# Square roots with a constant offset, two units in one instruction, and new instruction lists in a fused gated-recurrence and soft-MoE kernel

## The chip, the core and the metric

The kernel runs on one core of one Trainium2 chip. The metric is the device time of one execution in microseconds. Of the kernel before, three runs were timed: 292.63, 292.97 and 293.97, with a median of 292.97.

## What is computed

The input is a sequence model's layer followed by a soft mixture of experts. x, r_gate and i_gate are 4 x 5056 x 256 floats, and a_param holds one value per channel.

```python
log_a = 8 * sigmoid(r_gate) * log(sigmoid(a_param))
a_t = exp(log_a)
x_gated = sqrt(maximum(1 - a_t * a_t, 1e-6)) * sigmoid(i_gate) * x
h = a_t[:, t] * h + x_gated[:, t]          # for every t; y[:, t] = h
logits = y @ phi                           # 20224 tokens x 32 slots
slot_input = softmax(logits, over tokens).T @ y
slot_out = relu(slot_input @ w1[e]) @ w2[e]     # 8 experts, 4 slots each
out = softmax(logits, over slots) @ slot_out
```

The softmax over tokens needs all tokens, so the work falls into a first phase over all of them, a short middle (the two expert layers) and a last phase that writes 20.7 MB of output.

## The kernel before

**Tiles.** The 20224 tokens are cut into 40 quads of 512 (the last has 256). Quads are put together in 21 units: quad 0 alone, then pairs, then quad 39 alone. A big buffer, tag "b", holds one unit: 128 partitions (channels) x 2 halves of the 256 channels x 1024 tokens; there are 20 of them, made as ten tiles of two neighbours (line 579). Units are worked off in nine chunks of 2, 2, 3, 3, 3, 3, 2, 2 and 1 (CHUNKS, line 24), because ACT has to load another function table for the square root and batches the roots of one chunk between two loads.

**Steps of the first phase, by task name** (unit p or quad q behind it, and a half of the channels after the dot):

- Dr, Di, Dx: loads, issued by SP (line 728).
- TR: PE turns the r gate round to channels by tokens. SR: ACT takes tanh(r/2) into the buffer A (line 812).
- SI: ACT takes tanh(i/2) in place (line 827). The gate is sigmoid = (1 + tanh)/2, so what follows forms (1 + tanh) x, which is twice the gated input. A letter of IV (line 32) says how for each quad: P adds the 1 on POOL (P1, line 838) and multiplies on DVE or POOL (U, line 850); D does both in one DVE instruction (line 848); E multiplies only, and PE adds the two transposes (TU, line 922) in PSUM.
- EX: ACT takes the exponential of A (line 880), where two units of a chunk stand in neighbouring buffers in one instruction of 2048 elements. SQ: POOL or DVE squares it into N (line 867).
- RT: ACT takes the root of N in place (line 903). Since the gated input is doubled, the root is of (1 - a*a)/4, with an offset that is read from a tile called quarter.
- ST: DVE multiplies the root into the transposed input in PSUM (line 940). SC: DVE's scan along the tokens (line 957). It goes unit after unit, each from where the one before ended.
- TY: PE turns y round again (line 980). YC: DVE or ACT copies it to SBUF (lines 996 and 994).
- LG, LE, LD, TE, ES, AC, AE, DM: logits of a group of up to four quads, the running maximum, exponentials relative to it, the sum of slot inputs, and its rescaling when the maximum grows (lines 1042 to 1131).

**The middle.** merge_tasks (line 1297) brings the four partition blocks' running maxima to one: MT transposes them, MX and MR reduce and replicate, MC transposes back, WJ subtracts, WE takes the exponential, W scales the rows of a matrix R. SP and DN add the blocks up with it, SL and RD copy out and invert the sum. L1 (line 1375) and L2 (line 1423) are the expert layers, 128 matmuls each; HS, HT and HR copy, transpose and rectify between them, for four experts at a time. SO, RS and BD spread the result.

**The last phase.** For each group: CT, CM, CS, CE, RR, RB, RC and CN form the softmax over slots (partly done early), HP and HE turn it round, OT multiplies, OE copies to SBUF on DVE or ACT, OD stores.

**What sets the order.** The order of tasks on each of the five queues is written out by hand in ORDER (line 91). A planner (line 249) replays the lists with estimated durations to decide which buffer each task gets (take, line 473); all waits come from the data and the buffers. Each engine works strictly in the order of its list. Buffers that a double exponential is to use are "mates", which the planner takes together as two free neighbours (twin, line 455).

Of the kernel before, what the change touches and what calls it, by code (L numbers as in the profile page):

```python
# [17 lines left out]
P = 128  # L18
J = 4
# [12 lines left out]
IV = 'PDPDDDEPEPPEPDEPPPEEDEPEEDEDPEPPPPPEDPPP'  # L32
# [74 lines left out]
    ),  # L107
    "ACT": (
# [13 lines left out]
    ),  # L122
# [16 lines left out]
    ),  # L139
    "POOL": (  # L140
# [6 lines left out]
    ),  # L147
# [8 lines left out]
    ),  # L156
}
SWITCH = 0.09
WARMF = 1.4
COLD = 5.6  # L160
COLDB = 0.95
MARGIN = 0.25
COLDT = 3.3
COLDW = 3.4
FEW = 2.0
COLDX = 1.9
LOAD = 1.41

EX2 = True

MI = ()
RT2 = ()
SPR = 1.28
ISSUE = 0.45
AHEAD = 0.96
LATE_DMA = 0.2
PEX = 1.03

ODS = 0


# [24 lines left out]
class Buf:  # L206


    __slots__ = ("tags", "tag", "slot", "users", "name", "need", "late", "mate", "kept")

    def __init__(self, tags, name=""):
        self.tags = tags if isinstance(tags, tuple) else (tags,)
# [8 lines left out]
class Planner:  # L221
# [219 lines left out]
    def tag_for(self, b, taken={}):  # L441
        for g in b.tags:
            if b.kept is not None:
                return g
# [1218 lines left out]
```

## Time and profile before

| | |
|---|---|
| median of three runs | 292.97 us |
| profiled execution: its own time | 292.97 us |
| profiled execution: span from first to last instruction | 291.2 us |
| granted TensorE clock, mean | 0.968 of full speed |
| busy: PE, DVE, ACT, POOL | 253.9, 241.4, 241.4, 180.7 us |
| moved by DMA | 100.07 MB, 79 of them read |
| first output store issued | 237.79 us after the span's start |

All times below are in microseconds from the span's start, if nothing else is said. A row of the timeline joins instructions of one kind that follow one another; "x2" says how many, and the duration runs from the first one's start to the last one's end. In brackets stands how long the engine sat idle before, and what ended that. Successive ACT instructions overlap a little in the rows: the next one's start comes some 0.1 us ahead of the last one's end.

### The profile page before, as it was taken

To read this page: it belongs to the slowest core of one execution; us is meant where nothing else is said; L and a number is where in the kernel's file an instruction comes from. 1 tells how busy PE (TensorE), PEld (TensorE's weight loads), DVE (VectorE), ACT (ScalarE), POOL (GpSimd) and SP (SyncE) were. 2 spreads that over 40 slices of the span, in tenths; PEclk is the share of its full clock that TensorE was granted. 3 is DMA by queue.
4 is the path that set the end of the run, shared out by engine and by line. 5 is a ranking of instruction groups with operands and counts; after the bars stand their busy time and mean duration, and the time that the engine had idled before them with its cause. 6 is when DMAs were issued, how large, how long until landed. Compare 5 with 4: busy or idle time off the path is not lost.

```text
span 291.2 us, 6478 instructions
## 1 busy us (share of the span) xinstructions
PE 253.9 (87%) x2602; PEld 200.1 (69%) x2602; DVE 241.4 (83%) x277; ACT 241.4 (83%) x268; POOL 180.7 (62%) x138
## 2 busy tenths in 40 slices
PE   8997796897989999999998999999999999968620
PEld 7997685676876787777777677777675677746300
DVE  0059999999999999999999999999975558998530
ACT  4999999999999999999999999999842059866400
POOL 4344795798799999969999999997002021130100
PEclk9999999999999999999999999999999999999755
DMA  7999999999999998798859959999993029999996
GB/s 237 409 409 409 410 399 410 405 409 394 344 407 407 356 396 283 270 350 306 288 182 342 308 201 365 369 421 416 424 414 151 2 87 415 411 423 411 420 421 268
DMA packets 23634, 100.07 MB, mean 344 GB/s; under 512 B 2866, under 2 KB 2868, under 8 KB 19636
## 3 DMA queue, kind: packets, MB, share of 16 engines
q1 hardware_dynamic: 23600, 99.66, 88.1%
q8 instruction: 20, 0.33, 0.4%
q14 instruction: 10, 0.08, 0.1%
q10 hardware_dynamic: 4, 0.00, 0.0%
HBM read 78.94 MB, written 20.71 MB: 342 GB/s over the span
## 4 chain that ended last, share of the span: by engine, by line
ACT 39%; PE 27%; DVE 22%; issue 7%; POOL 1%; POOLq 0%; DVEq 0%; ACTq 0%
ACT b L880 9%; ACT b L812 9%; ACT st L827 9%; DVE b L957 8%; DVE pair L940 5%; ACT b L903 5%; PE bank L1590 5%; PE pair L922 3%; PE bank L1423 2%; PE pair L980 2%; ACT L903 2%; DVE b L1604 2%; PE one L1116 2%; DVE yn L996 2%; ACT yn L994 2%
## 5 line engine op out<-in xcount | busy, mean ns | idle before, releaser
L867 POOL TENSOR_TENSOR b<-b 128x1024 f32<-128x1024 f32 (+2 forms) x38 | 67.9, 1803 | 16.4 <-ACT b L880 15.2
L957 DVE TENSOR_TENSOR_SCAN b<-b,b,pair 128x1024 f32<-128x1024 f32 (+3 forms) x26 | 51.7, 2000 | 0.2
L940 DVE SCALAR_TENSOR_TENSOR pair<-b,pair 128x1024 f32<-128x1024 f32 (+2 forms) x42 | 48.0, 1154 | 4.4 <-ACT b L903 3.6
L801 PE MATMUL pair<-ident,st 128*128 128x128 f32 x316 | 42.2, 277 | 7.1 <-ACT b L812 2.9
L922 PE MATMUL pair<-ident,b 128*128 128x128 f32 x316 | 43.2, 274 | 4.0 <-ACT b L812 2.3
L1528 POOL TENSOR_TENSOR b<-b,rs_all 128x512 f32<-128x512 f32 (+3 forms) x12 | 10.7, 895 | 57.2 <-DVE rs_all L1525 54.9
L980 PE MATMUL pair<-ident,b 128*128 128x128 f32 x316 | 43.6, 282 | 2.2 <-ACT b L812 1.8
L850 POOL TENSOR_TENSOR b<-st,b 128x1024 f32<-128x1024 f32 (+1 forms) x18 | 42.6, 2374 | 3.9 <-DMA b<-in_x_dram 3.5
L980 PEld LDWEIGHTS pair<-ident,b 128*128 128x128 f32 x316 | 38.1, 193 | 9.6 <-ACT b L812 3.6
L880 ACT ACTIVATE b<-b,ca 128x2048 f32<-128x2048 f32 (+3 forms) x28 | 44.3, 1602 | 0.0
L801 PEld LDWEIGHTS pair<-ident,st 128*128 128x128 f32 x316 | 35.1, 142 | 13.4 <-ACT b L812 5.4
L812 ACT ACTIVATE b<-pair 128x1024 f32<-128x1024 f32 (+1 forms) x40 | 39.7, 1014 | 3.8 <-PE pair L801 3.7
L957 DVE TENSOR_TENSOR_SCAN b<-b,pair 128x1024 f32<-128x1024 f32 (+5 forms) x22 | 41.3, 1886 | 0.1
L827 ACT ACTIVATE st<-st 128x1024 f32<-128x1024 f32 (+1 forms) x40 | 41.2, 1058 | 0.0
L922 PEld LDWEIGHTS pair<-ident,b 128*128 128x128 f32 x316 | 35.4, 140 | 6.6 <-ACT b L812 3.1
L903 ACT ACTIVATE b<-b,quarter 128x2048 f32<-128x2048 f32 (+2 forms) x21 | 39.2, 1902 | 0.1
L850 POOL TENSOR_TENSOR st<-st,b 128x1024 f32<-128x1024 f32 x11 | 27.8, 2524 | 3.7 <-ACT st L827 1.9
L838 POOL TENSOR_SCALAR st<-st,one_sb 128x1024 f32<-128x1024 f32 (+1 forms) x19 | 22.1, 1168 | 9.0 <-ACT st L827 8.9
L996 DVE COPY yn<-pair 128x1024 f32<-128x1024 f32 x21 | 25.3, 1211 | 0.1
L1590 PE MATMUL bank<-eS,lD 32*128 32x256 f32 x210 | 23.1, 423 | 2.4 <-ACT lD L1574 1.3
L1042 PE MATMUL one<-b,phi_sb 128*32 128x256 f32 (+1 forms) x328 | 24.2, 395 | 1.1 <-DVE b L957 0.8
L1246 PE MATMUL one<-ident 128*128 128x128 f32 x146 | 23.6, 284 | 1.4 <-POOL ident masks.py:199 1.4
(135 smaller groups left out, 414.6 us busy)
## 6 DMA issues: line engine op xcount, KB each, us to landing
st<-in_i_gate_dram SPq DMA_DIRECT2D x39, 512.0 KB, 6.1
b<-in_x_dram SPq DMA_DIRECT2D x39, 512.0 KB, 8.3
st<-in_r_gate_dram SPq DMA_DIRECT2D x38, 512.0 KB, 6.6
out_dram<-b SPq DMA_DIRECT2D x19, 1024.0 KB, 10.0
b<-in_moe_w_dram SPq DMA_DIRECT2D x12, 1024.0 KB, 12.5
st<-in_moe_w_dram SPq DMA_DIRECT2D x8, 512.0 KB, 10.0
st<-in_r_gate_dram SPq DMA_DIRECT2D x3, 256.0 KB, 3.8
out_dram<-st SPq DMA_DIRECT2D x1, 512.0 KB, 3.9
```

What stands on the lines that cost most here:

```text
L801: nc.tensor.transpose(out=o[:, m, :], in_=raw("r", q)[:, m * D + h * P : m * D + (h + 1) * P], identity=ident,)
L812: nc.scalar.activation(dst, t(rp)[:, :, :c], AF.Tanh, scale=0.5)
L827: nc.scalar.activation(v, v, AF.Tanh, scale=0.5)
L850: eng.tensor_tensor(out=o, in0=a, in1=b, op=ALU.mult)
L867: eng.tensor_tensor(out=t(Nb[p])[:, h, :c], in0=v, in1=v, op=ALU.mult)
L880: nc.scalar.activation(v, v, AF.Exp, scale=ca[:, h : h + 1], bias=ca[:, h : h + 1])
L903: nc.scalar.activation(v, v, AF.Sqrt, bias=quarter if f != 1.0 else f, scale=-f)
L922: nc.tensor.matmul(o[:, m, :], raw(nm, q)[:, m * D + h * P : m * D + (h + 1) * P], ident, is_transpose=True, start=(nm == nms[0] and m == ...
L940: nc.vector.scalar_tensor_tensor(v, w, 1e-3 if gate_of(quads(p)[0]) == "S" else 0.5e-3, v, op0=ALU.max, op1=ALU.mult)
L957: nc.vector.tensor_tensor_scan(dst, dst, flat()[:, s0:s1], init, op0=ALU.mult, op1=ALU.add)
L980: nc.tensor.transpose(out=flat()[:, b * D + h * P : b * D + (h + 1) * P], in_=token(t(A[p])[:, h, : plen(p)], p)[:, :, (b0 + b) * len(quad ...
L1590: nc.tensor.matmul(t(ops[j])[:, (k - k0) * D : (k - k0 + 1) * D], t(hT)[r, k * P : (k + 1) * P], t(bdb)[r, :D], start=True, stop=True,)
```

## The change

- The root is taken of 1 - a*a, with the constant 1.0 as its offset, and no longer of a quarter of it. So y comes out doubled. phi is halved once after its load (PH, on POOL), which leaves the logits as they were; the sum of slot inputs is doubled, and RD inverts twice the denominator.
- For p = 5, 8, 11 and 14, the roots of units p and p + 1 are one instruction of 4096 elements.
- All 20 big buffers are one tile, so an instruction over two units can use any two buffers: its access pattern steps from the one to the other. Mates and twin are gone, and the planner takes the buffer that has been free longest.
- In the merge, MB multiplies a 0/1 mask by the maximum, MC sums that over partitions with R (which puts the four blocks' maxima beside one another in every partition), MX takes their maximum, and WE takes the exponential with the running maximum as its offset. MT, MR and WJ are gone.
- IV and all five lists are new. E becomes D for quad 6 and P for 21 and 26; P becomes D for 7 and E for 22; D becomes P for 13. On DVE stand 19 YC and no longer 21, on ACT 21 and no longer 19.

```diff
-IV = 'PDPDDDEPEPPEPDEPPPEEDEPEEDEDPEPPPPPEDPPP'
+IV = 'PDPDDDDDEPPEPPEPPPEEDPEEEDPDPEPPPPPEDPPP'
...
+RT2 = (5, 8, 11, 14)
...
-        make("b", -(-N_B // 2), [P, 4, 2 * QT], sb)
-        T["b2"] = T["b"]
-        T["b"] = [b[:, i : i + 2, :] for b in T["b2"] for i in (0, 2)]
+        big = sb.tile([P, H * N_B, 2 * QT], F32, name="b")
+        T["b"] = [big[:, H * i : H * i + H, :] for i in range(N_B)]
...
+        nc.vector.tensor_reduce(out=jmask, in_=ident.rearrange("p (j s) -> p j s", s=32), axis=AX.X, op=ALU.max)
...
-            v = T["b2"][A[p].slot[0] // 2][:, h::2, :] if len(us) == 2 else t(A[p])[:, h, :c]
+            ks = sorted(A[u].slot[0] for u in us)
+            v = big[:, H * ks[0] + h : H * ks[1] + h + 1 : H * (ks[1] - ks[0]), :] if len(us) == 2 else t(A[p])[:, h, :c]
...
-                f = 1.0 if gate_of(quads(p)[0]) == "S" else 0.25
-                nc.scalar.activation(v, v, AF.Sqrt, bias=quarter if f != 1.0 else f, scale=-f)
+        def e_rt():
+            v = t(Nb[p])[:, :, :c]
+            if p in RT2:
+                k0, k1 = sorted(Nb[u].slot[0] for u in us)
+                v = big.rearrange("q (k h) n -> q k (h n)", h=H)[:, k0 : k1 + 1 : k1 - k0, :]
+            nc.scalar.activation(v, v, AF.Sqrt, bias=1.0, scale=-1.0)
...
-                    v, w, 1e-3 if gate_of(quads(p)[0]) == "S" else 0.5e-3, v, op0=ALU.max, op1=ALU.mult
+                    v, w, 1e-3, v, op0=ALU.max, op1=ALU.mult
...
+    t_half = add("POOL", "PH", 0.2, deps=[ld[("x", PHI)]], prio=-5,
+                 emit=lambda: nc.gpsimd.tensor_scalar(phi_sb, phi_sb, 0.5, None, op0=ALU.mult))
...
+        a = add("DVE", "MB", 0.1, deps=[LE[G], t_const2], prio=-60, lock=True, emit=lambda: nc.vector.tensor_scalar(
+            small["mb"], jmask, mm, None, op0=ALU.mult))
+        a = add("PE", "MC", 0.25, deps=[a], prio=-60, alloc=[mp], shape="R", emit=lambda: nc.tensor.matmul(
+            t(mp)[:, :J], R.rearrange("p j s -> p (j s)"), small["mb"], start=True, stop=True))
+        a = add("DVE", "MX", 0.1, deps=[a], prio=-60, uses=[mp], emit=lambda: nc.vector.tensor_reduce(
+            out=small["mg"], in_=t(mp)[:, :J], axis=AX.X, op=ALU.max))
+        a = add("ACT", "WE", 0.2, deps=[a], prio=-60, kind="exp",
+                emit=lambda: nc.scalar.activation(small["wj"], small["mg"], AF.Exp, bias=mm, scale=-1.0))
...
-            nc.vector.tensor_scalar(small["rd"], t(sp)[:, P : P + 1], 1e-9, None, op0=ALU.add)
+            nc.vector.tensor_scalar(small["rd"], t(sp)[:, P : P + 1], 1e-9, 2.0, op0=ALU.add, op1=ALU.mult)
```

Of the lists, the stretches that the prediction speaks of, each before and after, are these. They are cut out of the lists and their lines broken anew.

```text
DVE, start, before:  CA SQ1.0 SQ1.1 U0 ST0.0 U1 ST0.1 SC0.0 SC0.1 U3 ST1.0 ST1.1 SC1.0 SQ3.0 SC1.1
DVE, start, after:   CA SQ1.0 U0 SQ1.1 U1 ST0.0 ST0.1 SC0.0 SC0.1 ST1.1 YC0.0 SC1.1 ST1.0 SC1.0 U3
ACT, fourth chunk, before: RT7.0 RT8.0 RT9.0          after: RT7.0 RT8.0
POOL before it, before: SQ7.0 SQ8.0 SQ9.0 SQ7.1 SQ9.1 U14 SQ8.1 P115
POOL before it, after:  SQ7.0 SQ8.0 U14 SQ7.1 SQ8.1 SQ9.0 SQ9.1 P115
ACT, end, before: YC27.0 YC28.0 SI35 SI37 SI38 RT18.0 YC30.0 RT19.0 DM7 YC31.0 YC32.0 SI39
ACT, end, after:  SI39 EX18.1 YC27.0 YC28.0 SI35 ES7 SI37 SI38 RT18.0 YC30.0 RT19.0 YC31.0
PE, logits, before: TU2.0 TR10 TU2.1 LG0.0 LG0.1 TR11      after: TU2.1 TR10 LG0.0 TU2.0 TR11 LG0.1
DVE, merge, before: SC20.1 AE9 RR0 LE11 LD11 YC37.0 MX RR1 MR AE10 WJ AE11 W SL
DVE, merge, after:  SC20.1 AE9 LE11 LD11 MB RR0 YC37.0 MX AE10 W AE11 CM5 SL
PE, middle, before: MC CT6 CT5 SP DN CT2 L1.0 ... L1.7 HT0 CT3 HT1 L2.0 ... L2.7 HP0 HP1 RS0
PE, middle, after:  CT2 CT5 SP DN CT3 L1.0 ... L1.5 HT0 L1.6 L2.0 L2.1 L1.7 L2.2 HT1 L2.3 ... L2.7 HP1 HP0 RS0
```

## Rows read from the trace of the kernel before

**Rows 1.** The page: busy us, share of the span, instructions.
```profile
PE 253.9 (87%) x2602; PEld 200.1 (69%) x2602; DVE 241.4 (83%) x277; ACT 241.4 (83%) x268; POOL 180.7 (62%) x138
```

**Rows 2.** Windows: stretch, its us; busy us by engine; clock, DMA share, GB/s.
```profile
28.00:192.00 164.00, 150.38 (x1483) 120.76 (x1481) 162.10 (x132) 163.62 (x145) 148.04 (x82) 1.00 0.92 347
192.00:211.00 19.00, 18.61 (x208) 13.90 (x206) 18.77 (x23) 17.99 (x25) 10.00 (x10) 1.00 1.02 422
211.00:238.00 27.00, 26.48 (x369) 17.75 (x370) 15.76 (x41) 8.60 (x22) 3.27 (x4) 1.00 0.38 155
238.00:288.60 50.60, 33.78 (x354) 23.95 (x352) 34.95 (x73) 28.11 (x58) 7.77 (x9) 0.84 0.99 409
```

**Rows 3.** Timeline of ACT, 184 to 200 us: start, duration, line, operation, tiles.
```profile
189.98 2.03 ACT L903 ACTIVATE b<-b,quarter 128x2048 f32<-128x2048 f32 x1
...
196.32 1.91 ACT L994 COPY yn<-pair 128x1024 f32<-128x1024 f32 x2
198.12 0.64 ACT L827 ACTIVATE st<-st 128x512 f32<-128x512 f32 x1
```

**Rows 4.** Timeline of DVE, 186 to 200 us.
```profile
189.68 2.33 DVE L957 TENSOR_TENSOR_SCAN b<-b,pair 128x1024 f32<-128x1024 f32 x1
192.05 1.23 DVE L940 SCALAR_TENSOR_TENSOR pair<-b,pair 128x1024 f32<-128x1024 f32 x1
```

**Rows 5.** Groups by shape on ACT: count | busy us, mean ns | idle.
```profile
L903 ACT ACTIVATE b<-b,quarter 128x2048 f32<-128x2048 f32 x19 | 37.4, 2003 | 0.1
...
L1105 ACT ACTIVATE dm<-M 128x1 f32<-128x1 f32 x10 | 3.0, 301 | 0.0
...
L903 ACT ACTIVATE b<-b,quarter 128x1024 f32<-128x1024 f32 x1 | 1.2, 1152 | 0.0
...
L1151 ACT ACTIVATE ca<-ca 128x2 f32<-128x2 f32 x1 | 0.2, 204 | 0.0
```

**Rows 6.** Timeline of ACT, 28 to 44 us.
```profile
31.39 2.10 ACT L880 ACTIVATE b<-b,ca 128x2048 f32<-128x2048 f32 x1
...
39.47 3.91 ACT L903 ACTIVATE b<-b,quarter 128x2048 f32<-128x2048 f32 x2
```

**Rows 7.** Groups by shape on DVE: the copies of y.
```profile
L996 DVE COPY yn<-pair 128x1024 f32<-128x1024 f32 x21 | 25.3, 1211 | 0.1
```

**Rows 8.** Groups by shape on POOL.
```profile
L838 POOL TENSOR_SCALAR st<-st,one_sb 128x1024 f32<-128x1024 f32 x18 | 21.4, 1195 | 8.9 <-ACT st L827 8.9
...
L1528 POOL TENSOR_TENSOR b<-b,rs_all 128x64 f32<-128x64 f32 x1 | 0.3, 293 | 6.1 <-DVE rs_all L1525 6.1
```

**Rows 9.** Timeline of DVE, 214 to 219 us, in the merge.
```profile
216.30 0.48 DVE L1131 SCALAR_TENSOR_TENSOR accS<-accS,dm,bank 64x257 f32<-64x257 f32 x1
216.70 0.28 DVE L1317 TENSOR_SCALAR W<-R,wj 128x128 f32<-128x128 f32 x1
```

**Rows 10.** Timeline of PE's weight loads, 222 to 230 us, between the layers.
```profile
223.73 1.75 PEld L1375 LDWEIGHTS one<-b,yn 128*32 128x32 f32 x32
225.92 0.32 PEld L1401 LDWEIGHTS one<-ident,st 128*128 128x128 f32 x2 [0.44 <-issue]
226.14 0.57 PEld L1492 LDWEIGHTS bank<-ident,b 128*128 128x128 f32 x4
...
227.07 2.96 PEld L1423 LDWEIGHTS bank<-b,b 128*32 128x32 f32 x60
```

**Rows 11.** Timeline of DVE, 15 to 44 us.
```profile
21.60 0.69 DVE L940 SCALAR_TENSOR_TENSOR pair<-b,pair 128x512 f32<-128x512 f32 x1 [2.74 <-ACT b L903]
...
32.44 1.21 DVE L867 TENSOR_TENSOR b<-b 128x1024 f32<-128x1024 f32 x1
```

**Rows 12.** Timeline of POOL, 82 to 192 us.
```profile
87.26 1.90 POOL L867 TENSOR_TENSOR b<-b 128x1024 f32<-128x1024 f32 x1
...
184.08 2.54 POOL L867 TENSOR_TENSOR b<-b 128x1024 f32<-128x1024 f32 x1 [0.30 <-ACT b L880]
```

**Rows 13.** Timeline of ACT, 84 to 94 us.
```profile
87.61 5.80 ACT L903 ACTIVATE b<-b,quarter 128x2048 f32<-128x2048 f32 x3
```

More of the change, by code (lines that the diff above doesn't have):

```diff
@@ L169 @@
 EX2 = True
+RT2 = (5, 8, 11, 14)
 MI = ()
-RT2 = ()
 SPR = 1.28
@@ L206 @@
 class Buf:
-    __slots__ = ("tags", "tag", "slot", "users", "name", "need", "late", "mate", "kept")
+    __slots__ = ("tags", "tag", "slot", "users", "name", "need", "late")
     def __init__(self, tags, name=""):
@@ L216, in __init__ @@
         self.need, self.late = {}, None
-        self.mate = self.kept = None
 class Planner:
@@ L442, in tag_for @@
         for g in b.tags:
-            if b.kept is not None:
-                return g
             if b.late is not None and not b.late(self, g):
-                continue
-            if b.mate is not None and self.twin() is None:
                 continue
@@ L453, in tag_for @@
         return None
-    def twin(self):
-        free = self.slots["b"]
-        return next((i for i in free if i % 2 == 0 and i + 1 in free), None)
     def pe_busy(self, now):
@@ L474, in take @@
         b.tag = self.tag_for(b)
-        if b.kept is not None:
-            b.slot = [b.kept]
-        elif b.mate is not None:
-            i = self.twin()
-            b.slot, b.mate.kept = [i], i + 1
-            self.slots["b"].remove(i)
-            self.slots["b"].remove(i + 1)
-        elif b.tag == "b":
-            free = self.slots["b"]
-            i = min(range(len(free)), key=lambda i: (free[i] ^ 1) in free)
-            b.slot = [free.pop(i)]
-        else:
-            b.slot = [self.slots[b.tag].pop(0) for _ in range(b.need.get(b.tag, 1))]
+        b.slot = [self.slots[b.tag].pop(0) for _ in range(b.need.get(b.tag, 1))]
         if b.tag == "pair":
@@ L611 @@
         R = sb.tile([P, J, NS], F32, name="R")
-        ones = sb.tile([1, 1], F32, name="ones")
-        quarter = sb.tile([P, 1], F32, name="quarter")
+        jmask = sb.tile([P, J], F32, name="jmask")
         eps_sb = sb.tile([P, 1], F32, name="eps")
@@ L674, in e_const @@
             nc.gpsimd.memset(b.rearrange("p (j d) -> p j d", d=D + 1)[:, :, D : D + 1], 1.0)
-        nc.gpsimd.memset(ones, 1.0)
-        nc.gpsimd.memset(quarter, 0.25)
         nc.gpsimd.memset(one_sb, 1.0)
@@ L765 @@
             second |= set(full[1::2])
-    for p in second:
-        A[p - 1].mate = A[p]
-    twin_rt = {
-        p + 1 for p in RT2 if p + 1 < NP and chunk_of[p] == chunk_of[p + 1] and p in WIDE and p + 1 in WIDE
-        and plen(p) == plen(p + 1) == 2 * QT and (gate_of(quads(p)[0]) == "S") == (gate_of(quads(p + 1)[0]) == "S") and p not in [x + 1 for x in RT2]
-    }
-    for p in twin_rt:
-        Nb[p - 1].mate = Nb[p]
     yn = {q: Buf("yn", f"yn{q}") for q in range(NQ)}
@@ L888, in mk_rt @@
     def mk_rt(p):
-        c = plen(p)
-        wide = p in WIDE
-        if p in twin_rt:
+        if p - 1 in RT2:
             RT[(p, 0)] = RT[(p - 1, 0)]
             return
-        us = [p, p + 1] if p + 1 in twin_rt else [p]
-        for h in range(1 if wide else H):
-            def e_rt(h=h):
-                v = t(Nb[p])[:, :, :c] if wide else t(Nb[p])[:, h, :c]
-                if len(us) == 2:
-                    v = T["b2"][Nb[p].slot[0] // 2]
-                f = 1.0 if gate_of(quads(p)[0]) == "S" else 0.25
-                nc.scalar.activation(v, v, AF.Sqrt, bias=quarter if f != 1.0 else f, scale=-f)
-            RT[(p, h)] = add("ACT", f"RT{p}.{h}", (0.07 + 0.17 * (H if wide else 1) / H) * len(us) + 0.835 * c / 1024 * (H if wide else 1) * len(us),
-                             deps=[SQ[(x, h2)] for x in us for h2 in range(H)] if wide else [SQ[(p, h)]],
-                             prio=pos_u(p), emit=e_rt, uses=[Nb[x] for x in us], kind="sqrt")
+        c = plen(p)
+        us = [p, p + 1] if p in RT2 else [p]
+        assert p not in RT2 or plen(p + 1) == c == 2 * QT
+        def e_rt():
[4 more added lines that the diff above has]
+            nc.scalar.activation(v, v, AF.Sqrt, bias=1.0, scale=-1.0)
+        RT[(p, 0)] = add("ACT", f"RT{p}.0", 0.14 + 0.835 * c / 512 * len(us), deps=[SQ[(u, h)] for u in us for h in range(H)],
+                         prio=pos_u(p), emit=e_rt, uses=[Nb[u] for u in us], kind="sqrt")
     def mk_scan(p):
@@ L1049, in mk_group @@
                 lg = add("PE", f"LG{g}.{2 * gunits[g].index(p) + h}", w * (0.00184 if p >= WIDE_FROM and w > P else 0.0036),
-                         deps=[SC[(p, h2)] for h2 in range(h + 1)] + [ld[("x", PHI)]], gate=begun(lg),
+                         deps=[SC[(p, h2)] for h2 in range(h + 1)] + [t_half], gate=begun(lg),
                          prio=quads(p)[-1] + 1 - LGP + fin, emit=e_lg, alloc=[lp] if own else [],
@@ L1185, in roots @@
     def roots(k):
-        return [("RT", p, h) for p in chunks[k] if p not in twin_rt for h in range(1 if p in WIDE else H)]
+        return [("RT", p, 0) for p in chunks[k]]
     for k in range(NC):
@@ L1263, in late @@
             return st[("i", NQ - 1)].tag is not None and len(pl.slots["st"]) >= 2
-        return len(pl.slots["b"]) > sum(b.tag is None for b in [*A.values(), *Nb.values(), *xb.values(), *(ib[p] for p in ib if two_i(p)), *lSb, hz] if b.kept is None)
+        return len(pl.slots["b"]) > sum(b.tag is None for b in [*A.values(), *Nb.values(), *xb.values(), *(ib[p] for p in ib if two_i(p)), *lSb, hz])
     hz = Buf("b", "hTz")
@@ L1299, in merge_tasks @@
         if tc is not None:
-            for nm, sh in (("mmax", [1, 1, NS]), ("mrep", [1, J, NS]), ("wj", [P, 1]), ("W", [P, J, NS]),
+            for nm, sh in (("mb", [P, J]), ("mg", [P, 1]), ("wj", [P, 1]), ("W", [P, J, NS]),
                            ("rd", [P, 1])):
@@ L1304, in merge_tasks @@
         G = NGR - 1
-        a = add("PE", "MT", 0.2, deps=[LE[G]], prio=-60, alloc=[mp], shape="T",
-                emit=lambda: nc.tensor.transpose(out=t(mp)[:1, :P], in_=mm, identity=ident))
-        a = add("DVE", "MX", 0.36, deps=[a], prio=-60, uses=[mp], emit=lambda: nc.vector.tensor_reduce(
-            out=small["mmax"][:, 0, :], in_=t(mp)[:1, :P].rearrange("o (j s) -> o s j", s=NS), axis=AX.X, op=ALU.max))
-        a = add("DVE", "MR", 0.21, deps=[a], prio=-60, lock=True, emit=lambda: nc.vector.tensor_copy(
-            out=small["mrep"], in_=small["mmax"].broadcast_to([1, J, NS])))
-        a = add("PE", "MC", 0.25, deps=[a], prio=-60, uses=[mp], shape="R", emit=lambda: nc.tensor.matmul(
-            t(mp)[:, P : P + 1], small["mrep"].rearrange("o j s -> o (j s)"), ones, start=True, stop=True))
-        a = add("DVE", "WJ", 0.1, deps=[a], prio=-60, uses=[mp], emit=lambda: nc.vector.tensor_tensor(
-            out=small["wj"], in0=mm, in1=t(mp)[:, P : P + 1], op=ALU.subtract))
-        a = add("ACT", "WE", 0.12, deps=[a], prio=-60, kind="exp",
-                emit=lambda: nc.scalar.activation(small["wj"], small["wj"], AF.Exp))
+        a = add("DVE", "MB", 0.1, deps=[LE[G], t_const2], prio=-60, lock=True, emit=lambda: nc.vector.tensor_scalar(
[6 more added lines that the diff above has]
+                emit=lambda: nc.scalar.activation(small["wj"], small["mg"], AF.Exp, bias=mm, scale=-1.0))
         w = add("DVE", "W", 0.2, deps=[a, t_const2], prio=-60, lock=True, emit=lambda: nc.vector.tensor_scalar(
```

109 rows, old and new, of the table ORDER are left out of this document.

## The prediction

> **What bounds the kernel now.** I read the busy table first [rows 1]: ACT and DVE carry equal loads, 241.4 us each, and PE 253.9. Such shares are means over unlike stages, so the windows come next [rows 2]. In 28 to 192 us ACT is busy 163.62 of 164.00 and DVE 162.10: neither has room. In 192 to 211 DVE is busy 18.77 of 19.00 and ACT no longer full. In 211 to 238 the DMA engines are busy 38% of the time and PE runs the merge, the two expert layers and their transposes. From 238 on the DMA share is 0.99: 50.6 us of output in which compute hides. So the end is a sum: the time at which phase one ends, plus the merge, plus a fixed output. The output's own order is changed too, but while the queue is full that costs and gives nothing; its cover is gone only if a tile is later than its turn in the queue.
>
> Which of the two full engines sets phase one? The root of unit 18 runs from 189.98 to 192.01 on ACT [rows 3]; the product with it, ST18, begins on DVE at 192.05, just when DVE's scan ends (189.68 + 2.33 = 192.01) [rows 4]. Both arrive together. After that point DVE has 19 us of products and scans that need nothing more than what is ready. So ST18 starts at the later of two sums: ACT's instructions up to that root, and DVE's. Every part of the change is priced on both.
>
> **ACT, up to the root of unit 18.** The roots read their offset from a tile: a root of 2048 takes 2003 ns, one of 1024 takes 1152, hence 0.831 ns an element and 301 fixed. One element with an offset from a tile (the DM rescale) takes 301, two elements with the constant 1.0 (the logarithm) 204 [rows 5]. So a constant offset saves 0.10 us, ends 0 and 0.10. Ten single roots lie ahead of unit 18: 10 x 0.10 = 1.0 saved, and 0.1 on that root itself. Of two units' roots in one instruction the trace has none. Two take 3.91 together [rows 6]; one of 4096 with a constant is 0.204 + 4096 x 0.000831 = 3.61, 0.30 less. Ends: 3.40 (no fixed part) and 3.91 (nothing saved); I take 3.61, since two lengths of the same instruction give it. Four pairs: 1.20, between 0 and 2.0. Exponentials over two units exist already [rows 6]; that their buffers need not be neighbours changes no instruction, only which buffers a plan may use.
>
> Against this stand two copies of y (YC) that move from DVE to ACT ahead of the root: YC10, 12, 14 and 18 come, 9 and 15 go. Two take 1.91 and the next instruction starts 1.80 after them [rows 3]: +1.80. The last input gate (SI39) now stands ahead of the root and not behind it: +0.64 at most [rows 3]. Table loads stay nine clusters each way. Sum: 1.80 + 0.64 - 1.00 - 0.10 - 1.20 = +0.14 us. ACT has no idle to win back, so by ACT the root of unit 18 ends 0.1 us later than now.
>
> **DVE.** The two copies it loses are 2 x 1.21 = 2.42 us [rows 7]; its U and SQ are exchanged one for one (U6, U7, SQ2.1, SQ5.1 for U8, U13, SQ3.0, SQ4.0). By DVE, ST18 could start 2.4 us earlier; by ACT it cannot. I take the later one: the 2.4 us become waits of DVE for roots. From ST18 to the last scan its list holds the same instructions: 0.
>
> **POOL and PE.** POOL gets one more P1 (20 for 19), 1.20 us, and the halving of phi, 128x64, between nothing and the 1.20 of a 1024-element one, taken as the 0.29 of its only 128x64 instruction [rows 8]. POOL idles 16 us of the 164 [rows 2], so both are hidden; without that cover they delay squares, hence roots (second rival). The logit matmuls wait for that halving instead of phi's landing; behind the first of them on PE queue TU2.0 and TR11, so a late halving would hold up those and then DVE's ST2.0 and ACT's next gate. PE loses sixteen transposes (E units 12 to 10) and has cover. SP issues as many loads as before in a new order, with the last weight now w20; the DMA engines idle most of 211 to 238 [rows 2], so a late weight has room: 0.
>
> **The merge.** Seven steps become five. But the slot product needs the last accumulation too, and that ends at 216.78 while W ends at 216.98 [rows 9]: of the shorter chain at most 0.2 us shows, then the accumulation is late. I take -0.1, as the new DVE step MB and the same copy YC37 stand ahead of it. The half in phi and the doubled denominator cost no instruction but the halving: the 2 is the second operation of an addition already there.
>
> **Between the layers.** L1's last weight load ends at 225.48, L2's first is at 227.07: 1.59 us with an idle of 0.44 and eight transposes, four of them CT3 [rows 10]. The new list puts CT3 ahead of L1 and sets HT0 and HT1 among the matmuls, so that their copies are hidden; yet each then costs its own entry, 0.44 + 0.32, and return, about 0.1: 2 x 0.86 = 1.72 against 1.59, or, without CT3's 0.57 and with half an entry hidden behind running matmuls, some 0.2 less. Ends +0.2 and -0.6; I take -0.1. The Trainium skill ("TensorEngine Tiling (Array Packing)", Key Properties) says that a change of tiling mode drains the engine; by this rule alone two more changes at 0.44 less CT3's 0.57 give +0.3, and 293.2 in all. The 0.44 idle in this case's rows agrees. What is left, one reduction on DVE at the start (jmask), lies ahead of DVE's wait of 2.74 us for the first root [rows 11]: 0.
>
> **The sum.** +0.14 + 0 - 0.1 - 0.1 = -0.06 us on the profiled execution's 292.97 us (span 291.2), which is also the median: 292.9. A measurement of this kernel can tell about 0.5%, 1.5 us, from no change.
>
> **Rivals.**
> A. DVE sets phase one, ACT's instructions run closer than I add them up, and the 2.42 us come through: 292.97 - 2.42 - 0.2 = 290.3, less if U1, which the new list puts ahead of the first product, fills DVE's 2.74 us wait there [rows 11]. For it: DVE idles only 1.9 us of the 164. Against it: ST18 and root 18 meet to 0.04 us [rows 3, 4]. Chance 0.18.
> B. Slower: a pair root waits for its last square. Root 8 starts at about 89.54 (87.61 + 5.80/3), and the square that it needs ends at 89.16 (87.26 + 1.90): 0.38 us to spare [rows 12, 13]. Now all four squares must be there at that time. Beyond 0.38 us of lateness ACT stands still, one for one. A square that collides with DVE takes 2.54 and not 1.90 [rows 12]; with the halving that is 0.64 + 0.29 - 0.38 = 0.55 a pair, 2.2 us at four: 295.1. The skill's "GPSIMD Engine Reference" (Key points) names that contention, with DVE instructions that have two SBUF inputs; the 2.54 agrees. Chance 0.10.
> C. Slower by far: an instruction over two distant buffers is held until all between them is quiet, in fourteen exponentials and four roots, for a scan of 2.33 us [rows 4] each: 18 x 2.33 = 42 us, over 330. Against it: SQ3.0 ran at 32.44 on a row between those that the exponential at 31.39 to 33.49 was writing [rows 6, 11]. Chance 0.02.
> D. The constant costs as much as the tile. Then the pairs alone save, 4 x 0.20, and the sum is 1.80 + 0.64 - 0.80 - 0.2 = +1.44: 294.4. Against it: 204 and 301 ns [rows 5]. Chance 0.08.
>
> **Numbers.** The forecast has 0.62; its own bounds (pairs 0 to 2.0 where 1.2 is taken, the layers, the merge) run from 291.5 to 294.5. The range leaves out C, the lower part of A and the upper of B: 290.3 to 294.8. Faster by over 0.5%: A and 0.02 of the forecast, 0.20. Slower: B, C and a third of D, 0.15. Within: 0.65.
>
> **What would show it.** Right: 17 roots, singles near 1.90 and pairs near 3.61 us; ACT without a gap up to root 18, ST18 starting at its end near 192; DVE idle for ACT's roots some 2 us more in 28 to 192; the first output store within 0.3 us of now. Wrong: DVE full and ST18 well ahead of 192 (A); ACT waits for POOL (B) or for loads and scans (C); roots of 2.00 us (D).

## The result, and the profile after

The changed kernel is slower: 297.70 us median of six runs against 293.34 of six of the kernel before on the same chip, ratio 1.013 (95%: 1.0087 to 1.0174). A second comparison (run after_again below) gave 1.014 (1.0106 to 1.0175). The forecast was 292.9, its range 290.3 to 294.8. The first ratio leaves out the changed kernel's slowest execution, 300.88 us, as a slow one, which is why it isn't the quotient of the two medians.

That slowest execution was also the first one profiled; up to the root of unit 18 it agrees with a second one of 298.54 us within 0.7 us. The rows below are of the second. Line numbers moved: roots L866, exponentials L845, scans L919, ST L902, TY L942, logits LG L1004, YC L956 (ACT) and L958 (DVE), products U L812 (DVE) and L814 (POOL), squares L831. First the page's busy row [rows 1], then windows, their bounds moved by 5 to 6 us as the root of unit 18 has moved [rows 2]:

```profile
PE 256.0 (86%) x2569; PEld 198.4 (67%) x2569; DVE 243.4 (82%) x274; ACT 242.6 (82%) x267; POOL 179.3 (60%) x138
```

```profile
28.00:198.00 170.00, 152.95 (x1471) 119.52 (x1473) 163.76 (x130) 165.47 (x144) 148.78 (x85) 0.99 0.91 340
...
217.00:243.00 26.00, 25.59 (x360) 17.30 (x360) 16.64 (x45) 9.37 (x21) 5.41 (x7) 1.00 0.31 125
243.00:294.00 51.00, 33.97 (x358) 24.08 (x350) 34.28 (x67) 28.34 (x59) 5.40 (x7) 0.83 0.98 406
```

The totals have hardly moved. But the first stretch is 6 us longer; ACT is idle in it for 4.5 us and DVE for 6.2, where it was 0.4 and 1.9 of 164. Nothing is lost in the last two stretches. The prices of the roots came out as taken (ACT's groups by shape [rows 5]): 1.912 us for 1.90, 3.614 for 3.61.

```profile
L866 ACT ACTIVATE b<-b 128x2048 f32<-128x2048 f32 x11 | 20.9, 1912 | 0.1
L866 ACT ACTIVATE b<-b 128x4096 f32<-128x4096 f32 x4 | 14.5, 3614 | 0.8 <-POOL b L831 0.8
```

So the work is as predicted, and the loss is waiting; the granted clock of 0.99 in the first window, where it was 1.00, is taken up below. The waits of ACT from 88 to 194 us and of PE's weight loads from 88 to 197 (engine, tile, line, what it waited for: us, times, longest):

```profile
ACT b L776 <- PE pair L765: 1.4, 2, 0.9
ACT yn L956 <- PE pair L942: 0.9, 2, 0.7
ACT b L866 <- POOL b L831: 0.8, 1, 0.8
...
PEld pair L942 <- ACT b L866: 1.7, 1, 1.7
PEld one L1004 <- ACT b L845: 1.2, 1, 1.2
PEld one L1004 <- ACT b L866: 1.1, 1, 1.1
```

The last three are new in kind. PE's transposes of y and its logits wait for a root or an exponential of ACT, which write nothing that they read. The timelines (start, duration) of the clearest one, on ACT, PE's weight loads, DVE and POOL:

```profile
120.81 3.62 ACT L866 ACTIVATE b<-b 128x4096 f32<-128x4096 f32 x1
...
124.48 0.30 PEld L942 LDWEIGHTS pair<-ident,b 128*128 128x128 f32 x2 [1.66 <-ACT b L866]
...
121.35 2.39 DVE L919 TENSOR_TENSOR_SCAN b<-b,pair 128x384 f32<-128x384 f32 x2
...
125.75 1.23 DVE L958 COPY yn<-pair 128x1024 f32<-128x1024 f32 x1 [1.55 <-PE pair L942]
126.89 1.22 DVE L902 SCALAR_TENSOR_TENSOR pair<-b,pair 128x1024 f32<-128x1024 f32 x1
128.01 2.33 DVE L812 SCALAR_TENSOR_TENSOR b<-st,b 128x1024 f32<-128x1024 f32 x1
...
126.88 2.38 POOL L814 TENSOR_TENSOR st<-st,b 128x1024 f32<-128x1024 f32 x1 [1.14 <-ACT st L791]
...
141.84 3.28 DVE L812 SCALAR_TENSOR_TENSOR b<-st,b 128x1024 f32<-128x1024 f32 x1
...
141.65 2.38 POOL L814 TENSOR_TENSOR b<-st,b 128x1024 f32<-128x1024 f32 x1
```

The pair root of units 11 and 12 works on buffers 13 and 2. TY15 reads buffer 10, which is neither, and starts only when the root has ended. DVE's copy YC15 then waits 1.55 us for TY15, and the product U25 behind it falls on POOL's U23 and takes 2.33 us, U27 on U26 3.28, where such a product took about 1.21 at those places before. The scan at 121.35, which writes buffer 12, ran during the same root: not everything between the two buffers is held.

The program's own lists show why. Each wait names an engine and how many of its instructions must be done; seven waits of the changed kernel over the big buffers ask for more than the data need, all between ACT and PE, and each has an instruction over two distant buffers at one end. The kernel before has none of these.

```text
waits                      for                        buffers
RT5 (units 5, 6)           a TY on PE                 0 and 6;   TY reads 5
LG of unit 7 on PE         EX10.0 (units 10, 11)      0 and 12;  LG reads 9
EX10.1                     that LG on PE              0 and 12
RT11 (units 11, 12)        a transpose on PE          2 and 13;  it reads 3
TY15 on PE                 RT11                       2 and 13;  TY reads 10
LG of unit 12 on PE        RT14 (units 14, 15)        2 and 9;   LG reads 6
EX16.0 (units 16, 17)      that LG on PE              5 and 12
```

### The profile page after: what moved, and what is told of

It reads as the page before. It is cut to its first block, busy times and chain, and to the rows that moved or that the text cites. A ratio compares the mean times of both kernels' runs of the same rounds, so it can differ in the third digit from the quotient of the medians.

```text
span 299.1 us, 6413 instructions
## 1 busy us (share of the span) xinstructions
PE 255.8 (86%) x2569; PEld 198.1 (66%) x2569; DVE 244.8 (82%) x274; ACT 242.8 (81%) x267; POOL 178.4 (60%) x138
## 4 chain that ended last, share of the span: by engine, by line
ACT 33%; PE 33%; DVE 14%; issue 10%; DMA 4%; POOL 2%; SPq 0%; POOLq 0%; DVEq 0%; ACTq 0%
ACT st L791 7%; ACT b L776 7%; ACT b L845 6%; ACT b L866 6%; PE bank L1550 5%; PE pair L942 5%; PE pair L884 4%; DVE b L919 4%; DVE pair L902 4%; DMA st<-in_r_gate_dram 3%; PE one L1004 3%; PE bank L1383 2%; ACT yn L956 2%; PE pair L765 2%; PE one L1078 2%
## 5 line engine op out<-in xcount | busy, mean ns | idle before, releaser
L919 DVE TENSOR_TENSOR_SCAN b<-b,pair 128x1024 f32<-128x1024 f32 (+8 forms) x48 | 92.9, 1951 | 0.7
L831 POOL TENSOR_TENSOR b<-b 128x1024 f32<-128x1024 f32 (+2 forms) x38 | 67.2, 1787 | 22.5 <-ACT b L845 20.2
L765 PE MATMUL pair<-ident,st 128*128 128x128 f32 x316 | 43.6, 282 | 9.5 <-DMA st<-in_r_gate_dram 4.6
L902 DVE SCALAR_TENSOR_TENSOR pair<-b,pair 128x1024 f32<-128x1024 f32 (+2 forms) x42 | 48.1, 1154 | 4.3 <-PE pair L884 3.0
L814 POOL TENSOR_TENSOR b<-st,b 128x1024 f32<-128x1024 f32 (+1 forms) x19 | 43.9, 2320 | 10.5 <-DMA b<-in_x_dram 9.9
L942 PE MATMUL pair<-ident,b 128*128 128x128 f32 x316 | 43.6, 283 | 5.6 <-DVE b L919 3.4
L942 PEld LDWEIGHTS pair<-ident,b 128*128 128x128 f32 x316 | 38.0, 193 | 13.8 <-DVE b L919 4.4
L765 PEld LDWEIGHTS pair<-ident,st 128*128 128x128 f32 x316 | 35.9, 144 | 16.1 <-DVE b L919 4.8
L884 PE MATMUL pair<-ident,b 128*128 128x128 f32 x316 | 44.3, 279 | 0.9 <-DVE b L919 0.4
L845 ACT ACTIVATE b<-b,ca 128x2048 f32<-128x2048 f32 (+3 forms) x28 | 43.9, 1592 | 0.0
L866 ACT ACTIVATE b<-b 128x2048 f32<-128x2048 f32 (+3 forms) x17 | 36.8, 2186 | 0.9 <-POOL b L831 0.8
L814 POOL TENSOR_TENSOR st<-st,b 128x1024 f32<-128x1024 f32 x10 | 23.8, 2383 | 4.4 <-ACT st L791 3.0
L1004 PE MATMUL one<-b,phi_sb 128*32 128x256 f32 (+1 forms) x328 | 24.6, 395 | 1.6 <-ACT b L866 0.9
L958 DVE COPY yn<-pair 128x1024 f32<-128x1024 f32 x19 | 23.0, 1214 | 2.4 <-PE pair L942 2.3
L956 ACT COPY yn<-pair 128x1024 f32<-128x1024 f32 (+1 forms) x21 | 20.6, 987 | 4.5 <-PE pair L942 4.4
```

What stands on the lines that cost most here:

```text
L765: nc.tensor.transpose(out=o[:, m, :], in_=raw("r", q)[:, m * D + h * P : m * D + (h + 1) * P], identity=ident,)
L814: eng.tensor_tensor(out=o, in0=a, in1=b, op=ALU.mult)
L831: eng.tensor_tensor(out=t(Nb[p])[:, h, :c], in0=v, in1=v, op=ALU.mult)
L845: nc.scalar.activation(v, v, AF.Exp, scale=ca[:, h : h + 1], bias=ca[:, h : h + 1])
L866: nc.scalar.activation(v, v, AF.Sqrt, bias=1.0, scale=-1.0)
L884: nc.tensor.matmul(o[:, m, :], raw(nm, q)[:, m * D + h * P : m * D + (h + 1) * P], ident, is_transpose=True, start=(nm == nms[0] and m == ...
```

## The experiments

Ratios are to the kernel before, run beside it on the same chip. "Stretch" is ACT's time from the start of the root of unit 7 to that of unit 18, "idle" its idle time in it, both from the profile's timeline.

```text
kernel               ratio (95%)                stretch us   idle us
before               1                          102.37       0
after_again          1.0140 (1.0106 to 1.0175)  107.21       3.10
split_roots          1.0042 (1.0001 to 1.0084)  106.55       2.61
split_both           1.0063 (1.0021 to 1.0105)  104.70       0
lists_only           1.0142 (1.0068 to 1.0216)  105.80       0
renamed_clear        1.0045 (1.0014 to 1.0077)  103.44       0
renamed_far          1.0232 (1.0193 to 1.0270)  109.27       5.21
before_const         0.9948 (0.9908 to 0.9987)  101.35       0
before_const_merge   0.9960 (0.9934 to 0.9986)  101.39       0
old_lists_pairs      1.0167 (1.0127 to 1.0207)  103.67       2.15
old_lists_copy       1.0231 (1.0189 to 1.0273)  106.13       3.38
clear_work_back      1.0144 (1.0106 to 1.0183)  106.26       4.50
after_u_early        1.0122 (1.0053 to 1.0192)  106.08       2.30
clear_back_u_early   1.0090 (1.0048 to 1.0131)  105.20       3.54
```

**Are the waits the loss?** First the distant pairs were written as two instructions.

```diff
-            nc.scalar.activation(v, v, AF.Sqrt, bias=1.0, scale=-1.0)
...
+            for v in vs:
+                nc.scalar.activation(v, v, AF.Sqrt, bias=1.0, scale=-1.0)
```

> The changed kernel, with its lists, but three of the four pair roots (units 5, 11, 14: buffers apart) and the pair exponentials of units 10 and 16 written as two instructions, one for each buffer. Work added on ACT: 3 x (2 x 1.91 - 3.61) + 4 x (2 x 1.24 - 2.10) = 2.2 us. Theory W (an instruction over two distant buffers is ordered against everything that touches a buffer between them): the waits of PE for a root (1.66 us at 124.5, 1.10 at 157.3) and for an exponential (1.22 at 105.4) are gone, and with them the gaps of ACT behind them; the time falls in spite of the added work, to 294.5 to 296.5. Rival L (the new lists are slower in themselves): the waits may go, but the time stays at 297.7 or rises by up to 2.2, to 297.7 to 300.

> The changed kernel with only those three pair roots written as two instructions each; the pair exponentials stay over distant buffers. Added on ACT: 0.6 us. Theory W: the two PE waits for roots (1.66, 1.10 us) go, the one for an exponential (1.22 at about 105) stays: 295.5 to 297. Rival L: 297.7 to 298.5.

split_both has no such wait left, and ACT no idle time in the stretch. Its ratio gives 1.0063 x 292.97 = 294.8, in W's range, though its own median is 296.2 on a chip where the kernel before ran at 295.1. split_roots came out lower than W had it (294.2 by its ratio). That would make the roots' waits worth more than the two stalls seen on PE, but its interval overlaps that of split_both, so it isn't shown. In its profile a load of r_gate stopped PE for 1.9 us at 156 and the granted TensorE clock was 0.50 from 157.1 to 160.5, so its stretch is not the cleanest.

> The changed kernel's lists, with every root a single instruction whose offset is read from a tile (2.00 us each as before) and the exponentials of units 10 and 16 split: of the change only the lists, the buffers' rule, the merge and phi's halving are left. Against split_both 17 roots cost 0.09 more each and one pair is gone (0.2): +1.8 us of ACT. Theory W with lists that are worth nothing in themselves: 2.2 less than or equal to split_both plus 1.8, that is 296 to 298, and before plus the added exponentials (292.97 + 1.6 = 294.5) if the lists are as good as the old ones. Rival L: 299 or more.

1.0142 is 297.1, within W's range, though the interval reaches L's 299. The stretch has no wait in it and is 3.4 us longer than before, where two copies of y, a gate and the split exponentials add 1.80 + 0.64 + 1.52 = 4.0.

The clearest pair changes no instruction at all, only the numbers of the buffers:

```diff
-        b.slot = [self.slots[b.tag].pop(0) for _ in range(b.need.get(b.tag, 1))]
+        if b.tag == "b":
+            b.slot = [SLOT[b.name]]
+            self.slots["b"].remove(SLOT[b.name])
...
```

> The changed kernel, instruction for instruction and list for list, but with its 20 buffers numbered by a table so that the two buffers of a pair lie mostly side by side (distances 1 to 5) and no instruction over two buffers is ordered against work on a buffer between them (none of the seven such waits of the changed kernel is left). No work is added or taken. Theory W (those waits are what the change lost): ACT runs from the root of unit 7 to that of unit 18 in 102.5 to 103.5 us (107.8 in the changed kernel) and the time is that of the kernel before within 1.5 us, ratio 0.995 to 1.005. Rival L (the lists): as the changed kernel, ratio 1.010 to 1.016. Rival S (late squares hold the pair roots, ACT waits for POOL): as the changed kernel.

> The same instructions and lists once more, the buffers numbered so that the pairs lie far apart (distances up to 15): fifteen waits of this kind in place of seven. Theory W: slower than the changed kernel, some 0.5 us for each wait more, ratio 1.015 to 1.04. Rivals L and S: as the changed kernel, 1.010 to 1.016.

With no, seven and fifteen such waits the same instructions give 1.0045, 1.0140 and 1.0232: W holds. (The numbers also set which earlier use a buffer has to wait for; that the time goes with these waits both ways, and ACT's idle with it, is what speaks for them.) Without them ACT never waits in the stretch, S's late squares included. The windows from 88 to 198 us of the changed kernel, of renamed_clear (PE, PE's loads, DVE, ACT, POOL) in that order:

```profile
88.00:198.00 110.00, 101.62 (x1021) 78.38 (x1021) 106.73 (x88) 106.66 (x95) 101.68 (x59) 1.00 0.88 321
```

```profile
88.00:198.00 110.00, 105.33 (x1056) 81.44 (x1057) 107.67 (x90) 109.74 (x97) 106.45 (x60) 1.00 0.90 330
```

ACT has its 3.1 us back. And the two products on DVE, U25 and U27, take 1.22 each in renamed_clear's timeline:

```profile
127.11 1.22 DVE L827 SCALAR_TENSOR_TENSOR b<-st,b 128x1024 f32<-128x1024 f32 x1
...
140.61 1.22 DVE L827 SCALAR_TENSOR_TENSOR b<-st,b 128x1024 f32<-128x1024 f32 x1
```

They still overlap POOL's products, but here they start first, and POOL pays: U23 takes 2.90 us and U26, which starts 0.20 behind U27, 3.27, where such a product alone takes 2.38. In the changed kernel U26 starts 0.19 ahead of U27, and U27 pays. So the one that starts later is drawn out.

```profile
140.81 3.27 POOL L829 TENSOR_TENSOR b<-st,b 128x1024 f32<-128x1024 f32 x1
```

In renamed_far the pair exponentials, too, hold PE's transposes (waits of PE's weight loads, then of ACT):

```profile
PEld pair L957 <- ACT b L860: 4.8, 3, 2.1
PEld one L1019 <- ACT b L860: 2.7, 2, 1.5
PEld one L1019 <- ACT b L881: 2.2, 2, 1.1
```

```profile
ACT yn L971 <- PE pair L957: 2.3, 3, 1.2
ACT eS L1075 <- PE one L1066: 1.7, 1, 1.7
```

**The changed kernel, profiled again:**

> The changed kernel once more, for a ratio from the same chip as the two others of this call and a second profile of it. Theory W: as before, ratio 1.009 to 1.017; ACT from the root of unit 7 to that of unit 18 in 106 to 108 us; PE idle at a logit or transpose instruction until a root or an exponential of ACT ends, at the same places (LG at about 105, TY at about 124, LG at about 157 us). Rival (the first profile was a disturbed run and its waits are chance): the waits stand elsewhere or are gone.

The waits stand at 105.33, 124.48 and 157.30 us, as in the first profile.

**The parts that do not need distant buffers**, on the old lists. before_const changes the roots, phi and the denominator; before_const_merge also has the new merge.

```diff
...
-                nc.scalar.activation(v, v, AF.Sqrt, bias=quarter if f != 1.0 else f, scale=-f)
+                nc.scalar.activation(v, v, AF.Sqrt, bias=1.0, scale=-1.0)
```

> The kernel before, its own lists and adjacent pairs, with only the constant offset of the roots, phi halved on GpSimd (one entry PH in its list) and the doubled denominator. Each of 19 roots of 2048 drops from 2.00 to 1.91 us, 1.8 us up to the root of unit 18. If ACT alone sets phase one: 291.2. If DVE, which arrived at the same time as ACT, binds as soon as ACT gains: 292.5 to 293.3. Under both theories not slower than 293.5.

> The kernel before with the constant offset, phi halved, the doubled denominator, and the shorter merge with its matmul ahead of the last accumulations; lists otherwise as before, no pair roots, adjacent pairs of exponentials in ten tiles. before_const gave 0.9948 (0.9908 to 0.9987); the changed kernel's profile has 7.28 us from ES9 to W where before has 7.89, so 0.6 us less: ratio 0.990 to 0.996. If the shorter chain only meets the last accumulation earlier, as the prediction took it: as before_const, 0.993 to 0.997.

Both are faster than the kernel before, by 1.5 and 1.2 us. In the stretch ACT saves 1.02 and 0.98 us where 11 x 0.10 were counted. Ahead of it nothing is saved: from the first gate to the root of unit 7 the two take 81.55 and 81.11 us for 80.52 before. ACT waits there, in before_const for PE once and for two loads:

```profile
52.73 1.03 ACT L812 ACTIVATE b<-pair 128x1024 f32<-128x1024 f32 x1 [0.86 <-PE pair L801]
...
83.87 1.06 ACT L827 ACTIVATE st<-st 128x1024 f32<-128x1024 f32 x1 [0.31 <-DMA st<-in_i_gate_dram]
85.12 1.06 ACT L827 ACTIVATE st<-st 128x1024 f32<-128x1024 f32 x1 [0.19 <-DMA st<-in_i_gate_dram]
```

The window of the kernel before shows the DMA engines full in that time (share 1.02):

```profile
8.00:88.00 80.00, 68.74 (x635) 60.72 (x634) 68.50 (x53) 79.07 (x71) 57.18 (x32) 1.00 1.02 401
```

The new merge added nothing that can be told (ES9 to W, the factor that ends the merge, takes 7.85 us for 7.82 in before_const, where 0.6 less was expected), as the prediction had it for the shorter chain.

**Pair roots on the old lists**, in neighbouring buffers:

```diff
...
-RT10.0 RT11.0 YC15.0 RT12.0 SI23 ... RT13.0 RT15.0 YC20.0
+RT10.0 RT11.0 YC15.0 SI23 ... RT13.0 YC20.0
...
```

> The lists of the kernel before with all the rest of the change: the constant offset, phi halved, the shorter merge, the one large tile, and pair roots for units 11 and 14 (two of the four, the other two find no neighbouring buffers), all pairs in neighbouring buffers by a table. ACT up to the root of unit 18: 11 x 0.09 + 2 x 0.21 = 1.4 us less than before. Theory W: no wait of the new kind, so not slower than before_const; ratio 0.990 to 0.997, limited by DVE, whose work is unchanged. If pairs cost by themselves (rival S): ratio above 0.998, with ACT waiting for POOL ahead of the roots of units 11 and 14.

> As old_lists_pairs, and one copy of y (unit of work YC14) moved from DVE to ACT: ACT +0.95, DVE -1.21 us. ACT then saves 0.4 and DVE 1.2 against before up to the root of unit 18. If DVE limits old_lists_pairs, this is faster than it by 0.5 to 1 us, ratio 0.988 to 0.995; if ACT does, slower by up to 0.95.

Both missed. Two things in them were not meant: their lists have the merge's matmul behind the last accumulations (ES9 to W takes 9.2 us for 7.9), and their buffers are not the ones longest free. In old_lists_copy the granted TensorE clock was also 0.50 from 125.7 to 129.2 us, inside its stretch. But the timeline of ACT also shows rival B of the prediction at one place: POOL's list there has a P1 between the squares, and the pair root waits for the last of them.

```profile
118.14 1.92 ACT L888 ACTIVATE b<-b 128x2048 f32<-128x2048 f32 x1
120.97 3.62 ACT L888 ACTIVATE b<-b 128x4096 f32<-128x4096 f32 x1 [0.92 <-POOL b L849]
```

What moving YC14 costs by itself can't be read from them.

**What renamed_clear still loses**, and the collisions:

```diff
-SC9.1 YC13.0 ... SC10.1 LE4                (DVE)
+SC9.1 YC12.0 YC13.0 ... SC10.1 YC14.0 LE4
-RT10.0 YC12.0 RT11.0 ... SI24 YC14.0 EX13.0 ... YC25.0 SI39 EX18.1 ... DM7 DM8      (ACT)
+RT10.0 RT11.0 ... SI24 EX13.0 ... YC25.0 EX18.1 ... DM7 SI39 DM8
```

> renamed_clear with two copies of y (YC12, YC14) moved back to DVE and the last input gate (SI39) back behind the root of unit 19, so that ACT holds the same kinds of work ahead of the root of unit 18 as before. Theory: what renamed_clear still loses (1.0045) is the work that the lists put on ACT, 2.4 us by the prediction's own terms: then ratio 0.996 to 1.000, unless DVE, which gets 2.4 us and has 1.5 us of waits from 88 to 196 us, takes the end over: 0.999 to 1.003. Rival: the new order itself costs (the early gap at ES0, 1.1 us): stays at 1.003 to 1.007.

It came out slower than either expectation. DVE has no gap over 0.15 us between 72 and 216 us, ACT waits 4.50 us, and U25 and U27 collide again, without any wait on a distant buffer:

```profile
126.27 2.56 DVE L827 SCALAR_TENSOR_TENSOR b<-st,b 128x1024 f32<-128x1024 f32 x1
141.22 3.19 DVE L827 SCALAR_TENSOR_TENSOR b<-st,b 128x1024 f32<-128x1024 f32 x1
```

So with these lists the two copies can't go back: DVE is then the limit, as the prediction's 2.42 us would have it, and the collisions come on top. Two list steps were to take these away:

```diff
-CS0 YC15.0 ST10.1 U25 SC10.1 ... SC11.0 YC16.0 U27 ST12.1
+CS0 U25 YC15.0 ST10.1 SC10.1 ... SC11.0 U27 YC16.0 ST12.1
```

> The changed kernel with its buffer numbers fixed (the same seven waits on a buffer between) and two gate products of DVE one step earlier in its list: U25 ahead of YC15, where DVE waits 1.55 us for PE anyway, and U27 ahead of YC16. Theory C (the waits shift DVE onto POOL's products, and these collisions are the larger part of the loss): U25 and U27 take 1.21 us each, DVE gains 3.2 us and up to 1.2 of a wait, ratio 1.002 to 1.007. Theory W alone (the stalls of PE and ACT are the loss and the collisions only fill waits): ratio 1.010 to 1.015, DVE waits instead.

> clear_work_back (no waits of this kind, two copies of y and one gate back where they were) with the same two steps of DVE earlier. clear_work_back had ratio 1.0144, U25 at 2.56 us and U27 at 3.19. Theory C: both at 1.21, 3.3 us less on a DVE that had no gap, ratio 1.001 to 1.006. Rival (DVE's two added copies, 2.4 us, are the cost): at most 1 us less, 1.011 to 1.015.

Theory C here is that of the collisions, not the prediction's rival C. Its range was met in neither: 1.0122 lies in that of W alone, 1.0090 between the two. But the step worked only by half: U25 now fell on POOL's U21 (2.69 and 2.24 us), U27 took 1.70 and 1.32. From the root of unit 7, which lies ahead of the step, to the start of ST18 after_u_early takes 108.03 us for 109.16 in the changed kernel, with 1.22 us less in the two products; clear_back_u_early 107.33 for 108.58, with 2.19 less. So the step is worth 1.1 and 1.2 us of that stretch: the collisions count, whatever brings them about. By the ratios the first pair overlaps (1.0140, 1.0122), so how the changed kernel's loss divides between stalls and collisions stays open.

**What the two profiles with the step show by the way.** Ahead of the step their lists are those of the kernels that they were made from, yet from the first gate to the root of unit 7 both take 79.77 us, where the changed kernel takes 80.93 and renamed_clear 81.37. The difference is the granted TensorE clock. In seven of the ten profiles with the new lists it is 0.50 for 3.4 us that begin between 68.1 and 70.3 us: the lower of its two levels, 1.2 for 2.4 GHz; in renamed_far it falls at 42.6 us instead. The window at that place, in the changed kernel and in after_u_early:

```profile
68.70:72.10 3.40, 3.40 (x19) 3.40 (x18) 2.05 (x2) 2.65 (x3) 3.40 (x2) 0.50 0.86 284
```

```profile
68.70:72.10 3.40, 3.27 (x28) 3.04 (x29) 3.26 (x3) 3.40 (x6) 3.38 (x3) 1.00 0.84 305
```

The transposes of an r gate that begin there take 1.72 us for 1.10, and ACT's exponentials ES0 then wait for PE (changed kernel, then after_u_early):

```profile
68.41 1.72 PE L765 MATMUL pair<-ident,st 128*128 128x128 f32 x8 [1.62 <-DVE b L919]
...
72.41 0.98 ACT L1060 ACTIVATE eS<-one 128x384 f32<-128x384 f32 x2 [1.06 <-PE one L1051]
```

```profile
68.80 1.10 PE L780 MATMUL pair<-ident,st 128*128 128x128 f32 x8 [1.65 <-DVE b L934]
...
71.62 0.98 ACT L1075 ACTIVATE eS<-one 128x384 f32<-128x384 f32 x2
```

None of the five profiles with the old lists has the lower level there. PE sat idle for 1.62 us just before the clock fell, and for 1.65 us in after_u_early, where it did not fall. So what lowers it, and whether the new order brings it on, isn't shown, nor which of the executions without a profile had it.

## Why the prediction was wrong

**The step that failed** is the chance given to rival C, and the use of [rows 6, 11] against it. "An instruction over two distant buffers is held until all between them is quiet" was priced at 42 us and dismissed because SQ3.0 ran on a row between two that an exponential was writing. That row shows only that such an access does not hold DVE's. In all kernels here every such wait is between ACT and PE: the logits and transposes read every second, fourth or eighth column of a buffer, or two of every eight, while squares, scans and PE's transposes of raw input touch whole runs. That the stride is the reason is inferred, not tried. So C was right in kind and wrong in reach: seven waits, stalls of 1.1 to 1.7 us on PE, 3.1 us of idle on ACT, and collisions behind them. The sum put such waits at nothing. renamed_clear against after_again prices them at 0.0095 of the time, 2.8 us, by their intervals 1.4 to 4.2 (on different chips, each against the kernel before); between them lies nothing but buffer numbers.

**"PE ... has cover"** failed with it. PE's stall itself had cover; what it delayed had none: DVE's copy of y (1.55 us of waiting), and ACT's next gates and copies (0.4 to 0.9 us each).

**ACT's sum** held. From the root of unit 7 on its terms give +1.80 + 0.64 - 3 x 0.30 - 5 x 0.10 = +1.04; renamed_clear measures 103.44 - 102.37 = +1.07. Ahead of it they give -0.30 - 5 x 0.10 = -0.8; the two profiles at full clock there measure 79.77 - 80.52 = -0.75. In the changed kernel's profile and renamed_clear's the lower clock costs 1.2 and 1.6 us there, more than that gain and as much as all that renamed_clear still loses (1.0045, 1.3 us). With the old lists and the clock at 1.00 the gain did not come (81.55 and 81.11 for 80.52): "ACT has no idle" did not mean that ACT sets the pace there, and with faster roots it waited for PE and for loads.

**DVE's 2.42 us** did become waits, as predicted, and more: 7.5 us of gaps from ST0 to ST18 where there were 2.5. ST18 still starts just when the root of unit 18 ends:

```profile
195.72 1.91 ACT L866 ACTIVATE b<-b 128x2048 f32<-128x2048 f32 x1
...
197.67 1.23 DVE L902 SCALAR_TENSOR_TENSOR pair<-b,pair 128x1024 f32<-128x1024 f32 x1
```

**Rival B** happened at one pair in four (0.81 us ahead of RT14 in the changed kernel), and not in renamed_clear: it follows from what else runs late. **A and D** did not happen. **The tail:** ES9 to W fell by 0.6 us (7.89 to 7.27), W to SO0 grew by 0.3 (17.56 to 17.83), and the 54.2 us from the first output tile to the end of the span are 54.3: 0.2 us less in all, as taken, though the merge gave more and the layers less than their terms; that is luck. (The estimate beside the layers' term, +0.3 for two more changes of mode, makes 293.3 with the other terms, not 293.2.)

## What to carry to other kernels

When separate tiles are joined into one so that an instruction can reach two of them, compare the program's waits before and after: each one that asks for more than the data need is a stall that no price list shows, and renumbering buffers can take it away at no cost. Before a difference between two profiles is put down to the program, compare the granted clock of the same stretch. An engine that is never idle need not be the one that sets the pace: ask, stretch by stretch, what it would wait for if it were faster. And the price of a product on VectorE beside one on GpSimd holds only for the order in which the two start: let either slip by 0.4 us, and the other engine may pay.

## What was not expected of the hardware

A product of DVE with two operands in SBUF takes 1.21 us alone and up to 3.28 when it starts 0.19 us behind one of POOL's (U27 behind U26, which keeps its 2.38); when it starts 0.20 ahead, it keeps 1.22 and POOL's takes 3.27. The 2.07 and 0.89 us so added are both more than the 0.64 that the prediction counted for a collision, from POOL's side [rows 12]. The Trainium skill ("GPSIMD Engine Reference", Key points) says that GpSimd shares its SBUF interfaces with VectorE and contends with VectorE's instructions of two SBUF inputs; the rows agree and give the size here.
